# Four zero stores moved to Pool's queue, under the weight loads of a decode layer

## The chip, the cores and the metric

The kernel runs on one core of one Trainium2 chip. The metric is the device time of one execution in microseconds (us); the time given for a kernel is the median of several runs. The engines are called PE (matrix multiply), DVE (vector), ACT (scalar), Pool (GpSimd) and SP (sync, which here only issues transfers). Sixteen DMA engines move data between the chip's memory (DRAM) and the on-chip memory (SBUF).

## What is computed

The reference is one decode step of a parallel layer, forward and backward, in bf16: attention over a sliding window of a K/V cache beside a gated FFN, both fed by one layer norm.

```
xn  = layernorm(x)                       # x: 4 x 1 x 512
q   = (xn @ wq) as 32 heads of 128
k,v = the last 1024 of 4096 rows of the caches, 8 heads, each used by 4 query heads
p   = softmax(q k^T / sqrt(128));  attn = (p v) @ wo
ffn = (gelu(xn @ w_gate) * (xn @ w_up)) @ w_down     # 512 -> 1792 -> 512
y   = x + attn + ffn
outputs: y, and the gradients of x, both caches, wq, wo, w_gate, w_up, w_down
```

Batch is 4. The gradients of the caches have the caches' full shape, 4 x 8 x 4096 x 128 each. Only the last 1024 rows can differ from zero; the 3072 rows ahead of them must be written as zeros. That is 48 MB of zeros (32 stores of 1536 KB) out of 81.0 MB written.

## The kernel before, in words

The work is one long stream for one core.

**Start (L126 to L220).** Constants and masks are built, the layer norm is computed, and a tile of zeros, `ztile`, is filled by Pool (L191). Output gradients are spread into `dyBD` (memset by Pool at L214).

**Weight loads (L137 to L278).** SP issues, in this order, W_gate (two halves, `load_wg`), x, W_up (`wu_sb`), W_down (`wd_sb`), Wq (`wq_sb`), Wo (`wo_sb`), and the first K (`load_kv(0, 0, kap, "ka", nc.sync)`), and behind them the first zero stores (L279).

**Zero stores (`zeros`, L247).** `ztodo` lists 32 stores, each for two heads of one batch row of one cache gradient. `zeros(n, after, deep)` takes the next n of the list and issues each from SP. `behind` makes one store wait for the landing of an earlier one: here the one that was issued `deep` (3) stores before. With `after` given, each waits for that instruction or transfer too. So a store waits on its issuing engine, and whatever stands behind it on that engine waits as well.

**FFN (L281 to L383).** Forward, then backward. The two halves of dW_down are collected in SBUF tiles and stored by `result` (L341), which issues from Pool (L112). Then, for up and for gate (L346), `dh` is spread into a tile `dhs` (memset by Pool at L356), the weights are transposed by DVE (L363) and multiplied to give dx, and dW is computed and stored in two halves (L381). `aSP` is a second spread tile (memset at L299). All result tiles come from one ring of four buffers, `stage` (`stg_tile`, L101): the tmp tile of the gelu, two of dW_down, `dhr` of the up pass, two of dW_up, `dhr` of the gate pass, two of dW_gate, and so on through the attention. A tile may be written when the store that reads its buffer's last content has landed. `evac` (L82) puts the copies out of PSUM on ACT or DVE by a running estimate of load.

**Attention (L390 to L648).** The second and later K and V tiles are loaded by Pool (`load_kv(..., nc.gpsimd)`), each into a buffer that the last use must have freed. For each of four batch rows: scores of q with K, and of the output gradient with V (`scores`), softmax, output (`odq`), dV (`dvdk(0, ...)`), softmax backward, dq (`odq(1, ...)`), dK (`dvdk(1, ...)`). `dvdk` stores 2 x 1 MB through Pool. Groups of zero stores stand at fixed places: behind the first V (2, L391), the second K (3, L392), the next V of each row (2, 2, 4, L637), the next K (3, L645), and in the last row behind the softmax (3, L631), the output (2, L639) and dq (the rest, 4, L647).

**End (L650 to L745).** Output and dx, then dWo and dWq: 8 stores of 1 MB through Pool.

**What sets the order.** SP's instructions stand in program order (`manual_schedule`, L78). On the other engines a scheduler chooses the order from priorities (program order, K/V loads first) and its own estimate of what is ready. On the chip each engine runs its instructions strictly in the order chosen.

Of the kernel before, what the change touches and what calls it, by code (L numbers as in the profile page):

```python
# [12 lines left out]
BF16 = mybir.dt.bfloat16  # L13
U32 = mybir.dt.uint32
P = 128
# [3 lines left out]
def kernel(  # L19
# [24 lines left out]
    nc = tc.nc  # L44

    B, Sq, D = A_x.shape
# [5 lines left out]
    K0 = Sk - W  # L52
# [5 lines left out]
    FB = F // P  # L58
# [4 lines left out]
    FPB = F // 64  # L63
# [18 lines left out]
    def evac(out, in_, n):  # L82

        ca, cd = (190 + n) / 1.2, (130 + n) / 0.96
        eng = "act" if load["act"] + ca <= load["dve"] + cd else "dve"
        load[eng] += ca if eng == "act" else cd
        if eng == "act":
            return nc.scalar.copy(out=out, in_=in_)  # L88
        return nc.vector.tensor_copy(out=out, in_=in_)  # L89

    def t32(out, in_, n):
        load["dve"] += (130 + n) / 0.96
        nc.vector.transpose(out=out, in_=in_)  # L93

    def pairs(ap):
        return ap.bitcast(U32)

    def scratch():
        return scrp.tile([P, 1024], U32, name="scr", tag="scr")

    def stg_tile():  # L101
        return stage.tile([P, 4096], BF16, name="stg", tag="stg")

    def store(eng, out, in_, kind, apart, **kw):

        d = eng.dma_start(out=out, in_=in_, **kw)  # L106
        for k in apart:
            tc.declare_no_dep(d.ins, group=k, reason="stores write disjoint parts of the outputs")
        tc.add_to_no_dep_group(kind, d.ins)
        return d  # L110

    def result(out, in_):  # L112
        return store(nc.gpsimd, out, in_, "rest", ["zeros", "rest"], single_packet=True)

    def mm(out, lhsT, rhs, first=True, last=True, pos=None):
        kw = {} if pos is None else {"tile_position": pos}
        nc.tensor.matmul(out, lhsT=lhsT, rhs=rhs, start=first, stop=last, **kw)  # L117

    def bank(name, tag="w", shape=(P, 512), dt=FP32):
        pool = {"w": ps_w, "x": ps_x}.get(tag, ps_a)  # L120
        return pool.tile(list(shape), dt, name=name, tag=tag)
# [7 lines left out]
    ffn = ffn_open.__enter__()  # L129
# [58 lines left out]
    ZP = P // 2  # L188
# [38 lines left out]
    def load_kv(b, k, pool, tag, eng, **kw):  # L227
        d_, src = ((k_t, A_k_cache), (v_t, A_v_cache))[k]
        tl = pool.tile([P, G, J, Dh], BF16, name=tag, tag=tag)
        for hf in range(2):  # L230
            hs = slice(hf * G // 2, (hf + 1) * G // 2)
            with tc.high_priority():
                d = eng.dma_start(out=tl[:, hs].rearrange("p g j d -> p g (j d)"),  # L233
                                  in_=src[b, hs, K0:Sk, :].rearrange("g (m j) d -> m g (j d)", j=J), **kw)
        d_[b] = tl
        return d

    ZG = 2
    zsrc = bass.AP(tensor=ztile.tensor, offset=ztile.offset, ap=[[2 * ztile[:].ap[0][0], ZP], [0, ZG], [1, ZW]])
# [3 lines left out]
    def behind(ins, other):  # L243
        tc.add_manual_dep(ins, other.name,
                          mybir.DependencyInfo(mybir.DependencyClass.Sync, mybir.DependencyReason.DATA))

    def zeros(n, after=None, deep=3):  # L247

        for _ in range(n):
            og, b, g = ztodo.pop(0)  # L250
            z = store(nc.sync, og[b, g:g + ZG, 0:K0, :].rearrange("g (m j) d -> m g (j d)", m=ZP), zsrc, "zeros",
                      ["rest"])
            if len(zdone) >= deep:
                behind(z.ins, zdone[-deep].ins)
            if after is not None:
                behind(z.ins, after.ins)
            zdone.append(z)


    if True:  # L260
        wd_sb = ffn.tile([P, FB, D], BF16, name="wd_sb")

        def ft(name, dt=FP32):
            return ffn.tile([P, Q, FB], dt, name=name)

        def flat(t_):
            return t_[:].rearrange("p f c -> p (f c)")
# [2 lines left out]
        tmp = stg_tile()[:, 0:4 * 2 * F // NQ].bitcast(FP32).rearrange("p (t f c) -> p t f c", t=4, f=Q)  # L270
        x2, ua, th, h1 = (tmp[:, t] for t in range(4))
        a_b, dhu, dhg = (ft(n, BF16) for n in ("a_b", "dhu", "dhg"))
        wu_sb = ffn.tile([P, C, F], BF16, name="wu_sb")
        nc.sync.dma_start(out=wu_sb[:].rearrange("p c f -> p (c f)"), in_=B_w_up.rearrange("(p c) f -> p (c f)", c=C))
        nc.sync.dma_start(out=wd_sb[:].rearrange("p c n -> p (c n)"), in_=B_w_down.rearrange("(p c) n -> p (c n)", c=FB))
        nc.sync.dma_start(out=wq_sb[:].rearrange("p c n -> p (c n)"), in_=A_wq.rearrange("(p c) n -> p (c n)", c=C))
        nc.sync.dma_start(out=wo_sb[:].rearrange("p k n -> p (k n)"), in_=A_wo.rearrange("(p k) n -> p (k n)", k=KH))
        load_kv(0, 0, kap, "ka", nc.sync)  # L278
        zeros(4)  # L279

        for wsb, t_ in ((wg_sb, hg), (wu_sb, hu)):  # L281
            ps = bank("h_ps", "w", (P, FQ))
# [12 lines left out]
        TT(out=a_b[:], in0=gl[:], in1=hu[:], op=ALU.mult)  # L295
        aT = ffn.tile([P, FB, Q], BF16, name="aT")
        t32(aT[:], a_b[:].rearrange("p f c -> p c f"), FQ)
        aSP = ffn.tile([P, FB, P], BF16, name="aSP")
        nc.gpsimd.memset(aSP[:], 0.0)  # L299
        for q in quad:  # L300
            TS(out=aSP[q, :, q], in0=a_b[q].rearrange("p f c -> p c f"), scalar1=gmask[q, 0:1], scalar2=None,
               op0=ALU.mult)
# [43 lines left out]
        for wi, (wsb, dh, og) in enumerate(((wu_sb, dhu, out_7), (wg_sb, dhg, out_6))):  # L346
            dh_f = flat(dh)
            dhr = stg_tile()
            for a, q in enumerate(quad):
                ps = bank("rep_ps", "w", (P, FQ))  # L350
                mm(ps[:], rsum_b[q, :], dh_f[q, :], pos=(Q * a, 0))
                evac(dhr[:, a * FQ:(a + 1) * FQ], ps[:], FQ)
            dhP = scratch()[:, 0:FPB * Q].rearrange("p (f x) -> p f x", f=FPB)
            t32(dhP, pairs(dhr[:, 0:F]), 896)
            dhs = ffn.tile([P, FPB, 2, 4 * B], BF16, name="dhs", tag=f"dhs{wi}")
            nc.gpsimd.memset(dhs[:], 0.0)  # L356
            dhPb = dhP.bitcast(BF16).rearrange("p f (x r) -> p f r x", r=2)
            for a, q in enumerate(quad):
                nc.vector.tensor_copy(out=dhs[q, :, :, a * B:(a + 1) * B], in_=dhPb[q, :, :, 0:B])
            for ch in range(4):  # L360
                sc = scratch()
                n7 = FPB // 4
                t32(sc[:, 0:n7 * P].rearrange("p (k c n) -> p c k n", k=n7, c=C),  # L363
                    pairs(wsb[:])[:, :, ch * n7 * Q:(ch + 1) * n7 * Q], 896)
                sb = sc[:, 0:n7 * P].bitcast(BF16).rearrange("p (k n r) -> p k r n", k=n7, r=2)
                for k in range(n7):
                    for r in range(2):
                        c = nm % 4
                        mm(dxf_ps[Q * c:Q * c + 4 * B, :], dhs[:, ch * n7 + k, r, :], sb[:, k, r, :], nm < 4,
                           nm >= 4 * FPB - 4, (0, Q * c))  # L370
                        nm += 1
            dwg_v = og.rearrange("(p h c) f -> h p (c f)", h=2, c=2)
            for h in range(2):
                stg = stg_tile()
                for ci in range(2):
                    for a, q in enumerate(quad):
                        ps = bank("dwg_ps", "w", (P, FQ))
                        mm(ps[:], xn_b[q, 2 * h + ci:D:C], dh_f[q, :], pos=(Q * a, 0))
                        o_ = (ci * NQ + a) * FQ
                        evac(stg[:, o_:o_ + FQ], ps[:], FQ)  # L380
                result(dwg_v[h], stg[:, 0:2 * F])  # L381
# [3 lines left out]
    with tc.tile_pool(name="mid", bufs=1, reuse_waits="tile") as mid:  # L385
# [3 lines left out]
        selb = mid.tile([Q, 4, P], BF16, name="selb")  # L389
        with tc.tile_pool(name="att", bufs=1, reuse_waits="tile") as att:  # L390
            zeros(2, load_kv(0, 1, att, "va", nc.gpsimd, single_packet=True))  # L391
            zeros(3, load_kv(1, 0, att, "kb", nc.gpsimd, single_packet=True))  # L392


            D3 = [att.tile([P, B, DPB, Q], U32, name=n) for n in ("D3q", "D3d")]
# [227 lines left out]
            for b in range(B):  # L623
                S = scores(0, b)
                if b + 1 < B:
                    dP = scores(1, b)
                    refill(0, b + 1)
                    refill(1, b + 1)
                P_f, P_b, p_done = softmax(S)
                if b == B - 1:  # L630
                    zeros(3, p_done)  # L631
                    turn_wq()
                    dP = scores(1, b)
                pT = turned(P_b, 0)
                o_done = odq(0, b, pT)
                if b + 1 < B:
                    zeros((2, 2, 4)[b], load_kv(b + 1, 1, att, "va", nc.gpsimd, single_packet=True))  # L637
                else:
                    zeros(2, o_done)  # L639
                dvdk(0, b, spread(P_b, 0), rows[1])  # L640
                dS_b = softmax_d(P_f, dP)
                dST = turned(dS_b, 1)
                o_done = odq(1, b, dST)
                if b + 2 < B:
                    zeros(3, load_kv(b + 2, 0, (kap, att)[b % 2], ("ka", "kb")[b % 2], nc.gpsimd, single_packet=True))  # L645
                elif b == B - 1:
                    zeros(len(ztodo), o_done)  # L647
                dvdk(1, b, spread(dS_b, 1), rows[0])  # L648
# [127 lines left out]
```

## Time and profile before

| what | value |
|---|---|
| time, median of 3 runs | 283.15 us (282.53 to 283.21) |
| the profiled execution's own time | 283.66 us |
| its span (first to last instruction) | 281.3 us |
| granted PE clock, mean | 0.61 of full speed |
| busy share of the span: PE, DVE, ACT, Pool | 66%, 58%, 44%, 21% |
| moved by DMA | 112.21 MB, mean 399 GB/s |
| read from, written to DRAM | 30.93 MB, 81.01 MB |

The span is what the profiler saw of the program; the execution's time has 2.4 us around it. In the page, a line such as `L106 POOL DMA_DIRECT2D out_dram<-stg` names the source line, the engine, the operation and the tiles (output <- inputs); in square brackets stands the idle time of the engine before it and what ended it. Issues of transfers stand under the issuing engine: all stores are recorded at L106 and all K/V loads at L233, whatever called them, and the transfer itself goes on after the issue ("to landing"). q0 is the queue that Pool feeds, q1 the one that SP feeds. The view "timeline" lists instructions in order of time: start, duration, engine, line, operation, tiles. The view "chain of waits" follows the work that ended last back from the end.

### The profile page before, as it was taken

How to read it: one execution, taken by the hardware profiler on the slowest of the kernel's cores; microseconds unless marked ns; L12 is line 12 of the kernel's file. 1: busy time of each engine (PE TensorE's matmuls, PEld its weight loads, DVE VectorE, ACT ScalarE, POOL GpSimd, SP SyncE). 2: the span in 40 equal slices, each digit the busy share in tenths (PEclk: the TensorE clock that was granted, in tenths of full speed). 3: DMA queues.
4: the chain of work that ended last, by engine and by line, in shares of the span. 5: the costliest groups of instructions: out<-in, count | busy, mean ns of one | idle time of the engine just before them, and what ended most of it. 6: DMA issues, size and time to landing. Idle time of an engine off the chain costs nothing.

```text
span 281.3 us, 4405 instructions
## 1 busy us (share of the span) xinstructions
PE 184.8 (66%) x1733; PEld 75.0 (27%) x1733; DVE 162.6 (58%) x309; ACT 124.3 (44%) x245; POOL 60.2 (21%) x135
## 2 busy tenths in 40 slices
PE   0327899869354999559946642953357997944980
PEld 0102363233122624224311321321034232410210
DVE  1869748899796616445028350574396104495980
ACT  1133855720102489525724402722341768544880
POOL 8500110088182213130040060020020020200210
PEclk9999965558855557555555555555555557775555
DMA  7999999999999999999999999999989999999996
GB/s 251 422 445 438 396 392 416 431 425 414 389 430 424 426 364 400 314 379 416 421 406 395 428 429 412 351 430 429 424 354 423 420 404 398 401 412 404 410 384 250
DMA packets 17027, 112.21 MB, mean 399 GB/s; under 512 B 1384, under 2 KB 1648, under 8 KB 11376
## 3 DMA queue, kind: packets, MB, share of 16 engines
q1 hardware_dynamic: 6688, 66.46, 56.9%
q0 software_dynamic: 10176, 45.35, 41.2%
q8 instruction: 13, 0.21, 0.3%
q10 hardware_dynamic: 144, 0.13, 0.1%
q14 instruction: 6, 0.05, 0.1%
HBM read 30.93 MB, written 81.01 MB: 398 GB/s over the span
## 4 chain that ended last, share of the span: by engine, by line
DMA 32%; issue 14%; DVE 10%; PE 9%; ACT 4%; POOL 2%; POOLq 0%; ACTq 0%; DVEq 0%
DMA out_dram<-stg 19%; DMA va<-in_A_v_cache_dram 11%; DVE scr L93 6%; ACT stg L88 3%; PE dwq_ps L117 2%; DMA out_dram<-ztile 2%; PE od_ps L117 2%; PE sc_ps L117 1%; DVE stg L89 1%; POOL out_dram L106 1%; PE kv_ps L117 1%; DVE dqs L603 1%; PE dwo_ps L117 1%; PE es_ps L117 1%; DVE spr L502 1%
## 5 line engine op out<-in xcount | busy, mean ns | idle before, releaser
L88 ACT CAST stg<-kv_ps 128x512 bf16<-128x512 f32 x118 | 63.8, 602 | 57.5 <-DMA out_dram<-stg 29.6
L106 POOL DMA_DIRECT2D out_dram<-stg x30 | 19.7, 659 | 146.2 <-ACT stg L88 105.0
L117 PE MATMUL sc_ps<-scr,bd 128*32 128x256 bf16 x256 | 24.2, 396 | 21.8 <-DVE scr L93 21.8
L117 PE MATMUL kv_ps<-dm,spr 32*128 32x256 bf16 x128 | 28.5, 399 | 6.8 <-ACT stg L88 5.0
L117 PE MATMUL kv_ps<-qm,spr 32*128 32x256 bf16 x128 | 24.5, 371 | 12.1 <-ACT stg L88 11.6
L93 DVE STREAM_TRANSPOSE scr<-va 128x1024 uint32<-128x1024 uint32 x16 | 18.8, 1216 | 12.6 <-DMA va<-in_A_v_cache_dram 12.5
L117 PEld LDWEIGHTS <-spr 32*128 32x128 bf16 x256 | 12.1, 101 | 46.8 <-issue 42.4
L117 PEld LDWEIGHTS <-bd 128*32 128x32 bf16 x256 | 8.1, 107 | 34.7 <-issue 34.1
L88 ACT CAST stg<-dwg_ps 128x448 bf16<-128x448 f32 x26 | 12.5, 554 | 5.8 <-PE dwg_ps L117 3.4
L88 ACT CAST stg<-dwo_ps 128x512 bf16<-128x512 f32 x18 | 10.0, 588 | 11.2 <-PE dwo_ps L117 8.9
L117 PE MATMUL dwo_ps<-dy_b,oSP 32*128 32x512 bf16 x32 | 9.4, 522 | 7.8 <-ACT stg L88 6.6
L89 DVE CAST stg<-kv_ps 128x512 bf16<-128x512 f32 x10 | 6.6, 678 | 12.0 <-DMA out_dram<-stg 6.0
L93 DVE STREAM_TRANSPOSE scr<-ka 128x1024 uint32<-128x1024 uint32 x8 | 9.6, 1228 | 6.1 <-DMA ka<-in_A_k_cache_dram 3.9
L233 POOL DMA_DIRECT2D va<-in_A_v_cache_dram x8 | 6.0, 756 | 31.6 <-PE od_ps L117 27.7
L93 DVE STREAM_TRANSPOSE scr<-kb 128x1024 uint32<-128x1024 uint32 x8 | 9.8, 1231 | 5.1 <-DMA kb<-in_A_k_cache_dram 4.5
L117 PE MATMUL do_ps<-scr,dyBD 128*128 128x512 bf16 x32 | 10.2, 460 | 2.1 <-DVE scr L93 2.0
L117 PE MATMUL dwq_ps<-dqSP,xn_b 32*128 32x512 bf16 x32 | 10.7, 586 | 0.9
L588 DVE SCALAR_TENSOR_TENSOR odt<-od_ps,oms,odt 128x128 f32<-128x128 f32 x4 | 1.4, 340 | 17.2 <-ACT odt L587 17.0
L89 DVE CAST stg<-dwo_ps 128x512 bf16<-128x512 f32 x14 | 9.2, 680 | 3.5 <-issue 2.3
L89 DVE CAST stg<-dwq_ps 128x512 bf16<-128x512 f32 x15 | 9.9, 689 | 1.7 <-PE dwq_ps L117 1.4
L117 PEld LDWEIGHTS <-pT 128*32 128x32 bf16 x256 | 9.2, 140 | 5.2 <-ACT pT L88 2.3
L88 ACT CAST stg<-dwq_ps 128x512 bf16<-128x512 f32 x17 | 9.8, 585 | 1.3 <-PE dwq_ps L117 0.6
(196 smaller groups left out, 317.1 us busy)
## 6 DMA issues: line engine op xcount, KB each, us to landing
out_dram<-ztile SPq DMA_DIRECT2D x32, 1536.0 KB, 13.8
out_dram<-stg POOLq DMA_DIRECT2D x24, 1024.0 KB, 12.8
va<-in_A_v_cache_dram POOLq DMA_DIRECT2D x8, 1024.0 KB, 15.8
out_dram<-stg POOLq DMA_DIRECT2D x6, 896.0 KB, 10.9
wq_sb<-in_A_wq_dram SPq DMA_DIRECT2D x1, 4096.0 KB, 24.1
wo_sb<-in_A_wo_dram SPq DMA_DIRECT2D x1, 4096.0 KB, 34.7
kb<-in_A_k_cache_dram POOLq DMA_DIRECT2D x4, 1024.0 KB, 20.6
ka<-in_A_k_cache_dram SPq DMA_DIRECT2D x2, 1024.0 KB, 43.4
```

Of the source, the lines that this page charges most:

```text
L88: return nc.scalar.copy(out=out, in_=in_)
L89: return nc.vector.tensor_copy(out=out, in_=in_)
L93: nc.vector.transpose(out=out, in_=in_)
L106: d = eng.dma_start(out=out, in_=in_, **kw)
L117: nc.tensor.matmul(out, lhsT=lhsT, rhs=rhs, start=first, stop=last, **kw)
L233: d = eng.dma_start(out=tl[:, hs].rearrange("p g j d -> p g (j d)"), in_=src[b, hs, K0:Sk, :].rearrange("g (m j) d -> m g (j d)", j=J), **kw)
L502: TS(out=sp[:, :, a, :], in0=src[:].rearrange("p (j m) -> p j m", j=J), scalar1=amask[:, a:a + 1], scalar2=None, op0=ALU.mult)
L588: done = STT(out=t_[:], in0=ps[:, 1, :], scalar=mk[:, 1:2], in1=t_[:], op0=ALU.mult, op1=ALU.add)
L603: nc.vector.tensor_copy(out=dqs[q, :, :, :, a * B + b], in_=d3v[q])
```

## The change

`zeros` gets an argument for the issuing engine. Right after the first K's load, four zero stores are issued from Pool, with at most two in flight (`deep=2`: the third waits for the first to land, the fourth for the second), and then three from SP, where four were issued from SP. Three groups later get one store fewer: behind the second K 2 for 3, behind the fourth V 3 for 4, and the rest behind the last dq is 3 for 4. The list of 32 stores and its order stay. The memsets of `aSP` and of the two `dhs` tiles are moved in the program ahead of the weight loads, and so ahead of the new stores on Pool; each `dhs` now has a name of its own in place of a tag.

```diff
-    def zeros(n, after=None, deep=3):
+    def zeros(n, after=None, deep=3, eng=nc.sync):
 
         for _ in range(n):
             og, b, g = ztodo.pop(0)
-            z = store(nc.sync, og[b, g:g + ZG, 0:K0, :].rearrange("g (m j) d -> m g (j d)", m=ZP), zsrc, "zeros",
+            z = store(eng, og[b, g:g + ZG, 0:K0, :].rearrange("g (m j) d -> m g (j d)", m=ZP), zsrc, "zeros",
                       ["rest"])
             if len(zdone) >= deep:
                 behind(z.ins, zdone[-deep].ins)
...
+        aSP = ffn.tile([P, FB, P], BF16, name="aSP")
+        nc.gpsimd.memset(aSP[:], 0.0)
+        dhs_t = []
+        for wi in range(2):
+            dhs_t.append(ffn.tile([P, FPB, 2, 4 * B], BF16, name=f"dhs{wi}"))
+            nc.gpsimd.memset(dhs_t[wi][:], 0.0)
         wu_sb = ffn.tile([P, C, F], BF16, name="wu_sb")
...
         load_kv(0, 0, kap, "ka", nc.sync)
-        zeros(4)
+        zeros(4, deep=2, eng=nc.gpsimd)
+        zeros(3)
...
-        aSP = ffn.tile([P, FB, P], BF16, name="aSP")
-        nc.gpsimd.memset(aSP[:], 0.0)
...
-            dhs = ffn.tile([P, FPB, 2, 4 * B], BF16, name="dhs", tag=f"dhs{wi}")
-            nc.gpsimd.memset(dhs[:], 0.0)
+            dhs = dhs_t[wi]
...
-            zeros(3, load_kv(1, 0, att, "kb", nc.gpsimd, single_packet=True))
+            zeros(2, load_kv(1, 0, att, "kb", nc.gpsimd, single_packet=True))
...
-                    zeros((2, 2, 4)[b], load_kv(b + 1, 1, att, "va", nc.gpsimd, single_packet=True))
+                    zeros((2, 2, 3)[b], load_kv(b + 1, 1, att, "va", nc.gpsimd, single_packet=True))
```

## The prediction

> **What bounds the kernel now.** I read the page first, its slices and its queue table.
>
> ```profile
> DMA  7999999999999999999999999999989999999996
> GB/s 251 422 445 438 396 392 416 431 425 414 389 430 424 426 364 400 314 379 416 421 406 395 428 429 412 351 430 429 424 354 423 420 404 398 401 412 404 410 384 250
> ...
> q1 hardware_dynamic: 6688, 66.46, 56.9%
> q0 software_dynamic: 10176, 45.35, 41.2%
> ```
>
> The DMA engines are busy in nearly every slice, while PE has 66% of the span and DVE 58%. 112.21 MB at about 420 GB/s are 267 us of a span of 281.3. Idle DMA time is small: in the table by stretches of 5 us I add up some 7 us, of which 4.5 lie in the first and last five. So bytes moved from one time to another bring something only where the chain of compute no longer waits for them. q1 is SP's queue (weights, first K, all 32 zero stores), q0 is Pool's (other loads, results). Next, Pool's timeline and ACT's around 41 us.
>
> ```profile
> 8.84 1.74 POOL L356 MEMSET dhs<- 128x896 bf16 x2
> 30.44 0.70 POOL L106 DMA_DIRECT2D out_dram<-stg  x1 [19.85 <-ACT stg L88]
> 34.88 0.53 POOL L106 DMA_DIRECT2D out_dram<-stg  x1 [3.74 <-DVE stg L89]
> ...
> 57.40 1.52 POOL L233 DMA_DIRECT2D va<-in_A_v_cache_dram  x2 [3.84 <-DVE scr L93]
> ```
>
> ```profile
> 41.81 0.97 ACT L88 CAST stg<-dwg_ps 128x448 bf16<-128x448 f32 x2 [2.30 <-DMA out_dram<-stg]
> ```
>
> Pool is free from 10.6 to 30.4. The two stores at 30.44 and 34.88 are the halves of dW_down (L341); they take 11.3 and 9.7 us to land, at 41.7 and 44.6 (issues in windows around each). The tile ring `stg` has four buffers, so the sixth tile (second half of dW_up) needs the first store landed, and the seventh (`dhr` of the gate pass) the second. ACT's wait ends at 41.81, 0.1 us after the first landing; `dhr` is first written at 45.56, 1 us after the second. The FFN stage already runs on the edge of these two landings. Last, the chain of waits:
>
> ```profile
> 123.27 22.70 DMA va<-in_A_v_cache_dram
> ...
> 164.54 36.52 DMA out_dram<-stg
> ...
> 239.55 16.72 DMA out_dram<-stg
> ```
>
> After the FFN the chain waits for Pool's transfers, which share the engines with SP's zero stores. How they share is in the DMA view of 35 to 37 us (weight rows of 32 KB against store rows of 7 KB) and of 150 to 175 us (zero rows of 12 KB, 1536 KB in 128, against 4 KB packets):
>
> ```profile
> q1 hardware_dynamic: 22, 0.52, 70.8%
> q0 software_dynamic: 25, 0.18, 21.4%
> ```
>
> ```profile
> q1 hardware_dynamic: 684, 7.62, 71.9%
> q0 software_dynamic: 757, 2.90, 28.9%
> ```
>
> The queues take turns packet by packet, about equal in number, so larger packets get the larger share.
>
> **The memsets.** `aSP` and `dhs` are named earlier in the program, but in the trace they run at 7.23 and 8.84 already, behind `dyBD`, as nothing held them. Gain nothing, cost nothing; without the move they might stand behind a waiting zero store.
>
> **Four zero stores on Pool.** Issue costs 0.5 to 0.75 us each (L106 rows) on an idle Pool. Two go at 10.6; the third waits on Pool for the first to land, the fourth for the second. Behind them on Pool stands the store of dW_down at 30.44. Bytes: 4 x 1536 KB = 6.29 MB. SP alone moves 444 GB/s from 15 to 30 us, all the engines give, so these bytes push the weights back. Before, W_down landed at 18.1, Wq at 27.8, Wo at 38.9 (issue plus time to landing). No row shows a zero store on Pool; I take its packet as on SP, 12 KB. Against W_down's 14 KB rows it gets near half: W_down, 1.84 MB from 13.8 on at half of 430 GB/s, lands near 22, and the matmul that reads it (21.37) slips by 1. Against 32 KB rows, turn by turn, it gets 27% (12 of 44 KB); the 35 to 37 us row gave Pool 25% of the bytes where sizes alone say 18%; so 27 to 35%, 110 to 140 GB/s. Then store 2 lands near 32, store 4 is issued near 33 and dW_down just behind it. Weights up to Wo plus all four zero stores are done at 38.9 + 6.29 MB / 0.415 = 54. Then the first half of dW_down, 0.92 MB against K's 2 KB packets at 300 GB/s (1.20 MB in 38 to 42), lands at 55 to 57 instead of 41.7. ACT's stall of 2.3 becomes about 16: **plus 14**. The second half lands 3 us later, as much behind as the first. From the 14 I take 2 off, since DVE's transposes of W_up and W_gate can run ahead in the stall (DVE idles 3.47 and 1.31 us in 42 to 46) and PE's clock, 1.00 until 35 and 0.50 after 40, may be granted again: 12, and 1 for W_down. Bounds: Pool at half the engines throughout has its zeros done near 42 and the store at 47, plus 5; if the dW_down stores got ahead of stores 3 and 4 on Pool, plus 1 to 6; if the zeros got no share beside the weights, they would follow at some 350 GB/s after 38.9, until 57, and the store would land at 60, plus 18.
>
> The Trainium skill, "DMA: Bandwidth & Descriptors", section "SWDGE vs HWDGE vs iDMA", has packets of preferably at most 4096 B on Pool's path; an estimate by that, 11% beside 32 KB rows, leaves most zeros until after Wo and makes it 19 rather than 14. No run here shows it yet.
>
> **SP's early zeros, four before, three after.** The first waits for Pool's second to land. They lie behind K in SP's queue and fill it until about 75 us, as the four did until 71.6. Backlog at the end of the FFN: before, 15.9 + 6.3 + 5.5 MB needed less 22.9 moved by 57.4 (the table's rates) = 4.8 MB; after, 3 zeros more, 12 us more at 410: 4.6. So the first V and second K load meet the same crowd. Nothing either way.
>
> **One fewer behind the second K.** Its third store is issued at 89.78 and lies across the second V's load (94.34, landed 103.4 and 106.1), for which the chain waits 9.05. 1.57 MB are 3.75 us; PE is busy all of 100 to 110, so not all comes through: minus 2.5 (0 to -3.75).
>
> **One fewer behind the fourth V.** It is issued at 190.61 behind three others which land until 200.9, and lands at 205.95. The store the chain waits for lands at 201.06, before this one's turn. From there to 239 the chain runs on PE and ACT. Nothing (0 to -1).
>
> **One fewer at the last dq.** Four are issued from 233.2 to 242.2, landing until 257.0. The store at 239.55 shares with them until 256.27, where ACT takes up dW_o. With 1.57 MB less that lands 3.75 us sooner, and the tail of 25 us (evacuations and 8.4 MB of stores, both full) moves with it: minus 3.75 (-2 to -4).
>
> Sum: 12 + 1 - 2.5 - 3.75 = +6.75 on the profiled execution's 283.66 us (span 281.3 and 2.4 around it): 290.4. That execution lies 0.5 above the median of 283.15, so 290.
>
> **Rivals.** *Faster: the FFN isn't held.* The scheduler may put the dW_down stores ahead of the two waiting zero stores on Pool, and Pool's share may suffice for them to land by 44. Then the stall is 1 to 2 and the late relief of 6.25 stays: 283.15 + 2 - 6.25 = 279. It decides at a stall of 6.25. For it: Pool's order is made by a scheduler, not by hand, and loads were issued out of turn at 57.40. Against it: the zeros stand earlier in the program and Pool has nothing else for 20 us.
>
> *No change: the engines are full anyway.* Three zero stores more by the FFN's end, three fewer later, 11.3 us each way; if the chain waits for bytes throughout, the sum is near nothing: 283, with 281.5 to 286 around it. For it speaks the DMA line; against it, that one of the three late stores lies in a stretch that compute sets, and that the early ones hold up stores with four buffers. The Trainium skill, same page, section "Issuing engines are not separate DMA queues", says that DMAs from different engines interleave on the same 16 and a second issuer saves issue time alone; the trace agrees (both queues together 422 GB/s in 150 to 175, SP alone 445).
>
> *Worse.* Plus 15 to 18 in the FFN, 1 for W_down, relief of 2 to 4: 283.15 + 12 to 283.15 + 17, 295 to 300.
>
> **Chances.** Forecast (287 to 295) 0.55; no change 0.16; faster 0.25; worse 0.04. By the bound of 0.3%, about what a measurement can tell: faster (under 282.3) 0.25 and 0.03 of the case of no change, within 0.07 of that case, slower its last 0.06 with the 0.55 and 0.04. The range, 279 to 295, reaches to the faster rival and to the forecast's upper end; the forecast's own is 287 to 295.
>
> **What would show it.** Pool's timeline: zero stores at about 10.6, 11.3, near 21 and near 32, then dW_down at 33. ACT's wait for `out_dram<-stg` near 41 us grows to over 10; the first V's load is issued near 70 instead of 57.4. After the last dq stand three zero stores instead of four, and the chain's last DMA wait ends 25 us before the end, as now. A dW_down store that lands by 46 would make the prediction wrong, as would a V load issued before 62.

## The result, and the profile after

The changed kernel takes 288.28 us (median of 4 runs, 287.31 to 288.36) beside 283.18 for the kernel before: a ratio of 1.0161, with a 95% interval of 1.0127 to 1.0196. Forecast was 290.0, range 279 to 295, slower with a chance of 0.65. Ratios here and below are of the runs within 1.5% of the fastest of their kernel, medians of all its runs, so that a loss in us differs a little between the two (4.6 by the ratio here, 5.1 by the medians). The profiled execution took 288.36 us, with a span of 286.4 against 281.3: 5.1 us more.

The same slices and queue lines of the page after:

```profile
DMA  7999999999999999999999999999959999999786
GB/s 258 406 435 423 430 423 413 420 419 430 429 395 414 434 407 365 381 304 427 420 411 394 422 421 398 411 397 431 413 210 403 418 423 386 413 391 364 314 362 261
...
q1 hardware_dynamic: 6112, 60.17, 50.8%
q0 software_dynamic: 10752, 51.65, 45.8%
```

The bytes are the same, 112.21 MB; 6.3 MB went from q1 (SP) to q0 (Pool). The DMA line has new holes: a 5 in slice 30 (about 208 to 215 us) and 7, 8, 6 at the end, with 210 GB/s in the hole and 314 to 364 near the end. So the engines, full to the end before, now run short of work late: in the table by stretches of 5 us their share from 210 to 215 is 0.42, where before they were full, and from 200 us to the end their idle time adds up to some 8 us, against 3 before. The difference is about what the kernel lost.

Pool's timeline from 10 to 66 us:

```profile
10.54 1.54 POOL L106 DMA_DIRECT2D out_dram<-ztile  x2
27.89 0.62 POOL L106 DMA_DIRECT2D out_dram<-ztile  x1 [15.81 <-DMA out_dram<-ztile]
41.18 0.62 POOL L106 DMA_DIRECT2D out_dram<-ztile  x1 [12.66 <-DMA out_dram<-ztile]
41.79 1.62 POOL L106 DMA_DIRECT2D out_dram<-stg  x3
...
65.14 1.52 POOL L233 DMA_DIRECT2D va<-in_A_v_cache_dram  x2 [0.80 <-DVE scr L93]
```

Pool waits 15.81 and 12.66 us for its own zero stores. The dW_down store, ready at 31, is issued at 41.79, together with two more. In the DMA view the two dW_down stores land 15.5 and 17.8 us after their issues, at 57.3 and 60.1 (before: 41.7 and 44.6). ACT's timeline shows who waits for that:

```profile
57.34 0.97 ACT L88 CAST stg<-rep_ps 128x448 bf16<-128x448 f32 x2 [10.64 <-DMA out_dram<-stg]
```

The write is that of `dhr` in the gate pass, the seventh tile of the ring, and not, as before, that of dW_up's second half, which here waits for no store. Presumably it got a buffer that no store held; the profile leaves the buffers' numbers out. The first V load goes out 7.7 us later than before (65.14 for 57.40), the second V load 8.8 later (103.14 for 94.34), the fourth 7.6 (169.92 for 162.30); at the end 5.1 are left. This lag, by how much the same instruction is later than before, is used again below.

```profile
94.34 1.49 POOL L233 DMA_DIRECT2D va<-in_A_v_cache_dram  x2 [2.21 <-PE od_ps L117]
```

```profile
103.14 1.49 POOL L233 DMA_DIRECT2D va<-in_A_v_cache_dram  x2 [2.21 <-PE od_ps L117]
```

The first K also lands later, at 67.0 for 50.8, but nothing waits for it: DVE first reads it at 83.50. The chain of waits in the second half:

```profile
118.05 13.24 DMA ka<-in_A_k_cache_dram
...
148.47 8.52 DMA kb<-in_A_k_cache_dram
...
172.15 35.36 DMA out_dram<-stg
```

These are the same kinds of waits as before; what has gone is the last one, 16.72 us behind a store at 239.55. From 208 us on the chain has no transfer any more; it runs on PE, DVE and ACT.

### The profile page after: what moved, and what is told of

Its sections match the earlier page's. It is cut to its first block, busy times and chain, and to the rows that moved or that the text cites. A ratio compares the mean times of both kernels' runs of the same rounds, so it can differ in the third digit from the quotient of the medians.

```text
span 286.4 us, 4406 instructions
## 1 busy us (share of the span) xinstructions
PE 187.6 (66%) x1733; PEld 76.3 (27%) x1733; DVE 162.6 (57%) x309; ACT 124.6 (44%) x245; POOL 62.9 (22%) x139
## 2 busy tenths in 40 slices
DMA packets 17027, 112.21 MB, mean 392 GB/s; under 512 B 1384, under 2 KB 1648, under 8 KB 11376
## 3 DMA queue, kind: packets, MB, share of 16 engines
q1 hardware_dynamic: 6112, 60.17, 50.8%
## 4 chain that ended last, share of the span: by engine, by line
PE 27%; DMA 20%; DVE 13%; ACT 5%; issue 5%; POOL 1%; POOLq 0%; DVEq 0%; ACTq 0%
DMA out_dram<-stg 12%; PE kv_ps L117 9%; DVE scr L93 5%; DMA ka<-in_A_k_cache_dram 5%; ACT stg L88 4%; DMA kb<-in_A_k_cache_dram 3%; PE sc_ps L117 3%; PE od_ps L117 3%; PE dwq_ps L117 2%; PE ok_ps L117 2%; PE dwo_ps L117 2%; PE ob_ps L117 2%; DVE stg L89 2%; PE dxq_ps L117 2%; DVE wq_sb L93 2%
## 5 line engine op out<-in xcount | busy, mean ns | idle before, releaser
L117 PE MATMUL dwg_ps<-dhg,xn_b 32*128 32x448 bf16 x16 | 5.2, 540 | 8.9 <-ACT stg L88 8.9
L117 PEld LDWEIGHTS <-xn_b 32*128 32x128 bf16 x64 | 5.1, 108 | 21.5 <-issue 21.2
```

## Experiments

Two theories were to be told apart. The theory of the prediction: on Pool, dW_down's stores stand behind the zero stores, and this holds the FFN. The rival: the engines are full from the start, so that three zero stores more early push back whatever needs a transfer later, whichever queue they use.

### The memsets alone

Edit of the changed kernel: the zero stores as before.

```diff
-        zeros(4, deep=2, eng=nc.gpsimd)
-        zeros(3)
+        zeros(4)
```

(and the three later groups as before.)

> The moved memsets alone, with all zero stores as before the change. Theory (the dW_down stores stand behind zero stores in Pool's queue): 283 us, within 0.3% of before, first V load issued at 57 to 58, as the memsets run at the same time either way. Rival (the loss comes from another order of instructions that the moved tiles give): a good part of the 5 us, 285 to 288.

Measured: 283.71 us beside 283.67, ratio 0.9995 (0.9963 to 1.0026). The memsets and the tiles' new names cost nothing.

### Pool's queue alone: four zero stores on Pool, none on SP, later groups as before

```diff
-        zeros(4, deep=2, eng=nc.gpsimd)
-        zeros(3)
+        zeros(4, deep=2, eng=nc.gpsimd)
```

> The four early zero stores go from Pool, SP issues none early, and all later groups are as before: the same number of bytes early and late as before the change, only on another queue. Theory: the first dW_down store still lands near 57 instead of 42, the first V load is issued near 65, and with no relief later the time is 288 to 291. Rival (only bytes count, whichever queue): 283 to 284.

Measured: 289.21 us, ratio 1.0180 (1.0139 to 1.0221). As many stores as before go out early, in the same order, and yet it is 5.1 us slower by the ratio. The waits for transfers from 30 to 106 us:

```profile
ACT stg L88 <- DMA out_dram<-stg: 12.4, 1, 12.4
DVE stg L89 <- DMA out_dram<-stg: 9.3, 1, 9.3
```

The stall in the FFN is there, the first V load goes out at 65.39. Putting these stores on Pool is enough to cause such a loss. It does two things at once, though: they stand ahead of dW_down in Pool's queue, and they go out from 10.5 us on, beside the weights, where SP sends them behind the first K. Of the waits for weights in this stretch there is one, of 0.9 us for Wq, so it is the results' buffers that hold the FFN.

### The early bytes alone: seven early zero stores, all on SP

```diff
-        zeros(4, deep=2, eng=nc.gpsimd)
-        zeros(3)
+        zeros(7)
```

> Seven early zero stores as in the changed kernel and the same fewer later ones, but all from SP, behind the first K. Theory: dW_down lands at 42 and 45 as before the change, the first V load goes out at 57 to 59, the late relief stays: 279 to 282. Rival (the early bytes push everything back, whichever queue): 286 to 289.

Measured: 287.29 us, ratio 1.0127 (1.0086 to 1.0168). That the queue alone makes the loss fell here: dW_down lands at 41.3 and 44.2, and the first V load goes out at 57.01, all as before, and still the kernel is 3.6 us slower. The second V load goes out at 102.16, 7.8 later than before. The waits for transfers in the same stretch, the second V load, and the chain of waits:

```profile
DVE scr L93 <- DMA va<-in_A_v_cache_dram: 5.8, 1, 5.8
DVE scr L93 <- DMA kb<-in_A_k_cache_dram: 2.3, 1, 2.3
ACT stg L88 <- DMA out_dram<-stg: 2.3, 1, 2.3
```

```profile
102.16 1.49 POOL L233 DMA_DIRECT2D va<-in_A_v_cache_dram  x2 [2.21 <-PE od_ps L117]
```

```profile
59.27 33.39 DMA kb<-in_A_k_cache_dram
102.90 10.99 DMA va<-in_A_v_cache_dram
130.84 22.24 DMA va<-in_A_v_cache_dram
```

The FFN is free, but the first V and the second K, issued at 57 to 59, share the engines with three zero stores more. The second K takes 33.4 us (before: 23.0) and the DVE stands 5.8 us for V and 2.3 for K, where before it stood for neither. So the delay that the change shows in the FFN comes back one stage later when the FFN is spared. By the second V load the lag is 8.8 with both causes, 9.0 with the queue alone and 7.8 with the bytes alone: two ways to the same lag, not two lags that add up. (Each is read from a single trace, good to some 2 us, as the single stores below show.)

### dW_down's stores past the queue, from ACT

```diff
-            result(dwd_v[h], stg[:, 0:FB // 2 * D])
+            result(dwd_v[h], stg[:, 0:FB // 2 * D], nc.scalar)
```

(and `result` gets an argument for the engine; with it, the store goes out without `single_packet`, an option that the results' stores have otherwise.)

> The changed kernel with the two dW_down stores issued from ACT instead of Pool, so that they stand behind no zero store; the bytes and their times stay. Theory: they land by 47, ACT's wait of 10.6 us at 57 goes, the first V load goes out by 60, 280 to 284. Rival (the early bytes as such): as the changed kernel, 287 to 289.

Measured: 289.77 us, ratio 1.0226 (1.0186 to 1.0265), slower than the change itself. It doesn't isolate what it was made for. The first store lands at 50.9 instead of 57.3, not by 47, and Pool's timeline shows that the scheduler put four other results behind the K and V loads:

```profile
64.92 1.52 POOL L235 DMA_DIRECT2D va<-in_A_v_cache_dram  x2 [22.36 <-DVE scr L93]
...
67.92 2.15 POOL L106 DMA_DIRECT2D out_dram<-stg  x4
```

Pool stood 22.36 us for the V buffer with finished results behind it. That is another order, and no verdict on either theory.

### What one zero store costs at each place

In the kernel before, one store is left out at one place. The stores behind it in the list move up, so that the last 1.57 MB of one cache gradient stay unwritten.

```diff
+    ztodo.pop()
     zdone = []
...
-            zeros(3, load_kv(1, 0, att, "kb", nc.gpsimd, single_packet=True))
+            zeros(2, load_kv(1, 0, att, "kb", nc.gpsimd, single_packet=True))
```

(`drop_va3` has `(2, 2, 3)[b]`, `drop_first` has `zeros(3)` behind the first K, `drop_last` the `pop` alone.)

> The kernel before, with one zero store left out altogether: the group behind the second K has two instead of three, and the list loses its last store, so that 1.57 MB of one cache gradient stay unwritten. It prices the late relief at this place alone. The prediction's step: 2.5 us less (280 to 281). Rival (every byte costs its share, as the engines are full): 3.75 less, 279.5. Second rival (PE is full there): nothing.

> The same with one store left out behind the fourth V (three instead of four); the last store of the list stays unwritten. The prediction's step: nothing to 1 us less (282 to 283). Rival (every byte costs its share): 3.75 less, 279.5.

> The same with one store left out behind the last dq (three instead of four). The prediction's step: 3.75 us less (279 to 280). Rival: 2.5 less, as the changed kernel's lag shrinks by 2.5 us from the store ahead of dW_o to the end, since from there the tail runs on PE and ACT.

> The same with one store left out behind the first K on SP (three instead of four). Theory that the FFN and the first scores wait for no byte before the change: nothing to 1 us less (282 to 283). Rival (every byte costs its share, so that an early byte costs what a late one does): 3.75 less, 279.5.

| store left out | median, us | ratio, 95% interval | in us of 283.2 |
|---|---|---|---|
| behind the first K | 280.26 | 0.9877 (0.9834 to 0.9920) | -3.5 |
| behind the second K | 279.96 | 0.9879 (0.9828 to 0.9931) | -3.4 |
| behind the fourth V | 282.24 | 0.9948 (0.9925 to 0.9972) | -1.5 |
| behind the last dq | 280.82 | 0.9899 (0.9867 to 0.9931) | -2.9 |

Within the intervals, a store early costs as much as one behind the second K, near the 3.75 us that 1.57 MB take at 420 GB/s. The rival's price holds, and the theory that nothing waits for an early byte is out, though before the change the FFN and the first scores show next to no wait for a transfer. Where the time comes from shows in the chain with the early store left out, beside that of the kernel before (22.70 and 36.52):

```profile
122.61 20.50 DMA va<-in_A_v_cache_dram
161.64 35.54 DMA out_dram<-stg
```

Up to the second V load that kernel is no earlier than before (95.73 for 94.34). Neither figure is better than some 2 us: in the three traces whose work is the same up to there (the kernel before, and those with the store left out behind the fourth V and the last dq) this load goes out at 94.34, 93.69 and 95.75. The waits that follow are shorter, and the fourth V load is 2.9 us earlier (159.40 for 162.30). So, as far as one trace tells, the backlog is handed on from stage to stage until something waits for it.

### All four Pool stores at once

```diff
-        zeros(4, deep=2, eng=nc.gpsimd)
+        zeros(4, deep=4, eng=nc.gpsimd)
```

> The changed kernel with all four Pool zero stores issued at once (deep=4), so that Pool itself waits for no landing and dW_down is issued at 31 instead of 42, still behind all four in Pool's queue. Theory (the queue holds dW_down back): it lands at 55 to 58 as with the change, 287.5 to 289. Rival (Pool's waiting as an engine holds it back): it lands by 50, 284 to 286.5.

Measured: 288.67 us, ratio 1.0181 (1.0156 to 1.0207), the same as the change. In Pool's timeline the waits for zero stores are gone, and dW_down is issued at 30.63:

```profile
10.54 2.78 POOL L106 DMA_DIRECT2D out_dram<-ztile  x4
30.63 0.56 POOL L106 DMA_DIRECT2D out_dram<-stg  x1 [17.30 <-ACT stg L88]
```

It still lands at 57.8, and ACT waits 11.5 us. What counts for this landing is the bytes ahead in the queue, not the 28 us in which Pool itself stands.

### Two on Pool, two on SP, later groups as before

```diff
-        zeros(4, deep=2, eng=nc.gpsimd)
-        zeros(3)
+        zeros(2, eng=nc.gpsimd)
+        zeros(2)
```

> Two early zero stores on Pool and two on SP, later groups as before the change: as many early bytes as before, and half of the four on Pool. Theory (what stands ahead of dW_down in the queue decides; four there cost 5.5 us with the same bytes): dW_down lands near 49, the first V load goes out 1 to 4 us later, 284 to 287. Rival (only stores that wait on Pool do harm, and here none does): 283 to 284.

Measured: 282.89 us, ratio 0.9963 (0.9949 to 0.9978): a little faster than before, and of all kernels here with the full output the fastest. The theory's 284 to 287 was wrong. dW_down lands at 48.4 and 51.3, 6.7 us later than before, as expected, but the wait is short:

```profile
ACT stg L88 <- DMA out_dram<-stg: 1.2, 1, 1.2
```

and the first V load goes out at 57.49. The tile that was late before waits for no store here either, as with the change. The seventh is first written at 48.49, right behind the landing, and the FFN ends no later for it. So, with the tiles as they fall here, dW_down can land some 6 us later at no cost, where the prediction saw next to no slack. Why this kernel gains 0.4% is open: the profiled executions have the same span, 281.3, and no stretch stands out.

### The memsets left where they were

```diff
-        aSP = ffn.tile([P, FB, P], BF16, name="aSP")
-        nc.gpsimd.memset(aSP[:], 0.0)
-        dhs_t = []
-        for wi in range(2):
-            dhs_t.append(ffn.tile([P, FPB, 2, 4 * B], BF16, name=f"dhs{wi}"))
-            nc.gpsimd.memset(dhs_t[wi][:], 0.0)
```

(back at their places in the FFN, as before.)

> The changed kernel with the memsets of aSP and dhs left where they were in the program. The prediction's step said that they might then stand behind a waiting zero store on Pool. If the scheduler puts them there, aSP is filled near 42 instead of 9, dW_down starts that much later, and the time is 295 to 305; if it takes them ahead as before, 288 as the changed kernel.

Measured: 288.25 us, ratio 1.0155 (1.0131 to 1.0178), the same as the change. Pool's timeline:

```profile
32.91 0.62 POOL L106 DMA_DIRECT2D out_dram<-ztile  x1 [11.33 <-DMA out_dram<-ztile]
33.52 1.61 POOL L300 MEMSET aSP<- 128x1792 bf16 x1
35.05 1.65 POOL L357 MEMSET dhs<- 128x896 bf16 x2
```

They do stand behind the fourth store, and dW_down is issued at 45.42 instead of 41.79. The time is the same, but ACT's long wait is another one. It comes ahead of dW_down, for its products, and PE itself waits for Wq before them:

```profile
37.54 3.58 PE L117 MATMUL q_ps<-xnT,wq_sb 128*128 128x4 bf16 x128 [6.94 <-DMA wq_sb<-in_A_wq_dram]
```

```profile
41.60 6.01 ACT L88 CAST stg<-dwd_ps 128x512 bf16<-128x512 f32 x12 [12.21 <-PE dwd_ps L117]
```

The zero stores ahead started 3.3 us earlier, at 7.24, and the store lands at 56.8, as with the change; ACT then waits only 1.0 us for it and 1.9 for the second half. So the delay of the memsets lies where the FFN stood anyway, and my 295 was wrong: it added the one to the other. The first V load goes out at 67.16, 2.0 later than with the change.

### The other way round: three early, five behind the fourth V

```diff
-        zeros(4)
+        zeros(3)
...
-                    zeros((2, 2, 4)[b], load_kv(b + 1, 1, att, "va", nc.gpsimd, single_packet=True))
+                    zeros((2, 2, 5)[b], load_kv(b + 1, 1, att, "va", nc.gpsimd, single_packet=True))
```

> The other way round: the kernel before with one zero store fewer behind the first K (three) and one more behind the fourth V (five). Theory (a zero store costs 3.5 us early and 1.5 behind the fourth V, as single stores left out showed): 1 to 2 us less than before, 281 to 282.5. Rival (the fifth store there fills no idle time any more): 283 to 284.

Measured: 284.09 us, ratio 1.0035 (1.0006 to 1.0064). The rival holds: the fourth store there costs 1.5 us, the fifth by estimate some 4 or 5 (the 3.5 won early are gone, and 1.0 more by the ratio; the runs spread from 282.87 to 287.22). In its trace the results of around 205 us land 10 to 12 us later than before, and the first dWo store goes out 1.2 later.

## Why the prediction was right, and where its steps were not

The direction and the time held, 290.0 against 288.3, with the mechanism named: dW_down behind the zero stores, and a stall of ACT over 10 us. That the time came so near is in part luck: two terms of the sum were too large, the FFN's delay (13 for 7.7, or 8.8 by the second V load) and what came back after it (6.25 for 3.7), and in the sum they offset each other. Step by step:

**Sharing beside the weights.** Forecast 27 to 35% of the bytes for Pool. The DMA view of 28 to 40 us in the profile after, 32 KB weight rows against Pool's zero stores:

```profile
q1 hardware_dynamic: 130, 3.74, 72.1%
q0 software_dynamic: 128, 1.41, 27.8%
```

That is 27%: 29 of the packets are under 512 B, and the others are zero rows and weight rows in equal number. Beside W_down's 14 KB rows the prediction took near half; from 13 to 20 us it was 35%, and the numbers were not equal:

```profile
q1 hardware_dynamic: 128, 1.83, 68.4%
q0 software_dynamic: 81, 1.00, 33.3%
```

The Trainium skill, "DMA: Bandwidth & Descriptors", section "SWDGE vs HWDGE vs iDMA", has packets on Pool's path preferably at 4096 B or less; the measurement differs (1.41 MB in 128 packets, 11 KB each on average) and decides, and the stall of 19 us that followed from 4 KB did not come. With the lower end of the share the first zero store landed at 27.6 instead of near 21, the second at 40.9 instead of near 32, and the fourth was issued at 41.2 instead of 33.

**Landing of dW_down.** Forecast 55 to 57, measured 57.3. The sum of bytes ahead gave it, whatever the share; the run with all four stores at once gave 57.8 again.

**The FFN's delay, forecast at 13, measured at 7.7.** This is the first term that was mis-sized. ACT waited 10.64 us, 8.3 more than before, not 14 more, as dW_up's second half no longer hung on that landing. W_down's late landing, priced at 1, cost nothing: it landed at 20.3 instead of 22, ahead of its use. The prediction read from the 0.1 us between landing and ACT's restart that the stage has no slack, and took the same tile to wait after the change; the run with two stores on Pool shows about 6 us.

**SP's early stores, "nothing either way".** Wrong as a rule, right in this sum only because the FFN is late by as much. Without the FFN's stall (all seven on SP) the same bytes hold up the first V and second K, and the lag at the second V load is 7.8 all the same. The prediction had the rival of full engines at 0.16 and at no net loss; its mechanism alone costs 3.6. By the single prices, three stores earlier cost 3 x 3.5 = 10.5 and give back 3.4 + 1.5 + 2.9 = 7.8: an estimate of 2.7 for the loss, from prices uncertain by 0.7 to 1.5 each, where all on SP measured 3.6 (2.4 to 4.8 by its interval). The change lost 4.6 (3.6 to 5.6 by its interval). Whether Pool's queue, which alone costs 5.1, adds anything to that is not clear of noise.

**The late relief, forecast at 2.5, 0 and 3.75, together 6.25.** In the trace of the change the lag falls from 8.8 at the second V load to 5.1 at the end, so 3.7 came back, to some 2 us. This is the second term that was mis-sized. Left out alone, in the kernel before, the stores are worth 3.4, 1.5 and 2.9, together 7.8. The 3.7 are net of what the early stores may still have cost behind the second V load, where the prediction put nothing; the two were not taken apart. Behind the second K, PE's full stretch from 100 to 110 us hid little. Behind the fourth V the relief was not nothing. At the last dq it is below 3.75. The prediction expected the chain's last wait for a transfer to stay there, 25 us before the end; it is gone, and PE, DVE and ACT make up the chain in its place. The busy times of 15 us of the tail, each starting 21.3 to 21.4 us before the end, first of the kernel before, then of the one after (columns: us, then busy time and count of PE, PE loads, DVE, ACT, Pool, then PE clock, DMA share, GB/s):

```profile
260.00:275.00 15.00, 12.55 (x40) 2.77 (x37) 12.51 (x19) 11.91 (x21) 2.76 (x6) 0.50 0.98 400
```

```profile
265.00:280.00 15.00, 13.04 (x40) 2.89 (x39) 12.73 (x20) 12.68 (x23) 2.66 (x5) 0.50 0.83 341
```

PE, DVE and ACT are busy for some 12 to 13 of these 15 us in both, while DMA falls from 0.98 to 0.83. So the three were nearly full there before the change too, which would leave fewer bytes little to win; that is argued, not shown.

**The memsets: nothing.** Held: moved, they cost nothing (0.9995). Left in place they did end up behind a waiting zero store, as the prediction thought they might, and the time was the same, with the FFN's wait at another point.

**What stays open.** Why two stores on Pool and two on SP are 0.4% faster than all four on SP, and how much of the late relief came in the change. The loss of the change was not taken apart with a larger ring of result tiles, and dW_down past Pool's queue with the rest of the order unchanged wasn't reached either.

## What to carry to other kernels

Where the DMA engines are full, as here, a transfer that is moved earlier can cost its bytes at a later place where something waits for a transfer, even if the stage that it is moved into shows next to no wait; price a place by leaving one transfer out there and measuring. A filler on the queue that also carries results can set when the results' buffers come free, by its bytes ahead in that queue: here it made no difference whether the issuing engine itself waited. Two causes that end in the same lag need not add up: take each away alone before naming one.

## What the runs showed of the hardware that was not expected

Pool's transfers of 12 KB rows went out in packets of about that size (1.41 MB in 128 packets, some of them under 512 B), as SP's do. Against SP's 32 KB rows they got 27% of the bytes for 12 us on end, against 14 KB rows 35% for 7 us. All seven zero stores on SP's queue left the FFN untouched (dW_down at 41.3 us), four on Pool's did not (57.5): here the queue of a filler decided whom it held up, while the sum of both stayed at 403 GB/s from 13 to 20 us and 430 from 28 to 40.
